# Attention and an MLP mixer on one core: batch 0 loaded by ranges of tokens, its down projection by seven block products, in a new order

## The chip, the core and the metric

The kernel runs on one core of a Trainium2 chip. The core's engines work side by side: PE (TensorE) multiplies matrices into PSUM, DVE (VectorE) and ACT (ScalarE) copy, add and exponentiate, POOL (GpSimd) and SP (SyncE) mainly issue DMA transfers. The metric is the device time of one execution in microseconds (us); smaller is better. The profile is of one execution, whose own time is given beside the times of the other runs.

## What is computed

Eight batches, eight heads, 576 tokens of 64 channels. Attention is causal in blocks of 64 tokens; its output x (576 x 512 a batch) goes through a token mixer and a channel mixer:

```python
scores = scale * q @ k^T                  # block_i >= block_j, else -1e9
x = softmax(scores) @ v                   # per head; heads side by side: [8, 576, 512]
h = relu(x^T @ w_tok1) @ w_tok2           # 576 -> 256 -> 576, over tokens
u = x + h^T
out = u + relu(u @ w_ch1) @ w_ch2         # 512 -> 1536 -> 512, over channels
```

Inputs and output are float32 in HBM.

## The kernel before

Every piece of work is registered by `P.add(engines, cost, emit, deps, ...)` and gets the next number. The string `ORDER` then says in what order the pieces are issued and on which engine: `173Tsbc` is piece 173 on PE (T), with the PSUM places s, b and c; A is ACT, D is DVE, P is POOL, S is SP. Each engine runs its own pieces in this order and waits only where a tile is not ready or not free, so a load that stands early in POOL's order delays all that POOL issues behind it. The costs in `P.add` and the fields `prio`, `xfer` and `at` served the planner that wrote the string; at run time the string alone counts.

**Loads.** `load_qk(b, hg)` brings k and q of four heads (group hg). For batches 1 to 7 POOL issues one DMA each (L413) that casts float32 to bf16. The partition is (head, 32 groups of 18 tokens), so a run in HBM is 18 tokens. DVE then transposes 32 x 32 blocks (L436) into kT and qT, where 32 partitions hold one head. The raw buffer of a group is free for the next batch only when these transposes are done. For batch 0, group 0, SP loads k in float32 in two halves (L420) into the idle tile gT[0] (`k_stage`), ACT casts them (L395 by the helper `cast`), and POOL loads q in three pieces (L431); group 1 comes by POOL in halves. `load_v` (L462) has ten loads for batch 0 (five blocks of 128 tokens for each group) and five for the others. The weights follow on POOL: w_tok1 and w_tok2 (L473), w_ch1 in eight pieces f, m (L496), w_ch2 in three (L505).

**Batch 0's attention** (`first_attention`) runs before anything else can. Group and pair j (0 to 3) have three score sets n each: set 0 holds the blocks of tokens 256 to 575 against each other, sets 1 and 2 the others. `score_set` emits matmuls of 32 rows (L560). The first set covers all four heads of group 0. ACT takes exp of 1024 columns at a time (L578). The product with v (L608, and L661 for the last 64 tokens) is divided by its sum on DVE (L628, L634). Until there is work, PE multiplies zeros (`raise_clock`: WARM = 11 matmuls, L366, and single fillers, L373).

**Token mixer of batch 0**: `token_up` (L802, L806) and `first_uT` (L835, L850), which makes u transposed, uT, directly, so that u itself is not stored for this batch.

**Channel mixer.** `channel_up` (L1021), for batch 0 alone, has 12 products of four matmuls, each followed by relu. `channel_down_fast` (L1348) makes the down projection of the batches from 1 on by seven block products on half-size blocks (84 matmuls of 256 columns, four sums of blocks on DVE at L1330, six folds with the residual u at L1372). Batch 0 has `first_down` instead: for each of four row blocks four matmuls with the identity bring the residual from uT (L1439), and twelve of 512 columns the product (L1443); a cast and a store follow. `weight_sums` (L1300) makes the sums of w_ch2 that the block products need.

**Opening.** `init_tiles` fills constants on DVE (the ones and zeros of v1, the zeros for the warm-up, the bars of the mask) and the identity on POOL, which stands late in the order (12P, behind the v loads).

Of the kernel before, what the change touches and what calls it, by code (L numbers as in the profile page):

```python
# [9 lines left out]
FP32 = mybir.dt.float32  # L10
# [17 lines left out]
class Plan:  # L28


    TURN = {
# [22 lines left out]
    def add(  # L54
        self, engines, cost, emit, deps=(), prio=0.0, take=(), give=(), xfer=None, mode=0, at=0.0,
        urgent=0, until=1e9, quick=False, stick=False,
    ):

        o = Op()
        o.engines = (engines,) if isinstance(engines, str) else tuple(engines)  # L60
        o.cost = cost if isinstance(cost, dict) else {e: cost for e in o.engines}
        o.emit, o.prio, o.take, o.give, o.xfer = emit, prio, take, give, xfer
        o.mode, o.at, o.urgent, o.until, o.quick, o.stick = mode, at, urgent, until, quick, stick
        o.deps = list({id(d): d for d in deps if d is not None}.values())
        o.n = len(self.ops)
        self.ops.append(o)
        return o
# [30 lines left out]
    13S 9D 5D 16S 1D 43Ta 21P 2D 7D 11D 19P 10D 4D 3D 23P 31P 29P 14A 25P 15D 17A 33P 22D 18D 27P 20D 44Tb 249P 45Tb  # L98
    46Tb 47Td 24D 48Ta 49Ta 37P 50Ta 173Tsbc 36P 179Tt 174A 51Ta 52Ta 35P 53Ta 54Ta 55Ta 56Ta 57Ta 180A 34P 175D
    177Ts 26D 58Ta 59Ta 30D 176P 60Ta 178A 198Tt 252P 32D 61Ta 62Ta 40P 63Ta 199A 64Ta 28D 196Ts 42P 65Ta 66Ta 67Ta  # L100
    197A 230Tt 251D 258P 68Ta 69Ta 250D 70Ta 192A 39P 71Ta 211Ts 231A 189Td 38P 185Ta 186T 190D 181Tb 191D 182T 193A
    41P 232D 215Tt 212A 194D 154P 195D 72Tc 183D 73Tc 184D 200Td 74Tc 216A 75Tc 157P 213D 217Ts 8D 233D 254D 155P
    201T 218A 234Tt 187D 188D 12P 204Tb 214D 253D 205T 235A 255P 236Ts 206D 207D 156P 202D 227Ta 237A 203D 208Tb
    160P 223Tc 228D 224T 229D 219Td 159P 220T 225D 278Taefg 226D 161P 209D 210D 246Tc 221D 158P 222D 238Tb 281A 239T
    247D 162P 248D 242Td 279A 243T 240D 336Tc 163P 241D 282A 244D 334Ta 245D 280A 165P 260D 338Tb 335D 273Tdhfg 256D
    339A 342Ta 276A 340Tb 164P 277A 348Te 343T 341D 275A 337D 349T 399P 257D 351Tb 352T 350A 259D 263P 345Tc 344A
    346T 353D 274A 266Tfghe 262P 347D 267A 298Tabdc 261P 268A 356Tf 302A 265P 301A 360Tc 300A 357D 269A 358Td 361A
    354Tb 299A 270A 310Tcagf 355D 362Th 313A 271D 303D 272P 304D 312A 330D 264P 364Tb 363A 314A 396P 376Ta 311A 166P
    331D 370Te 359A 402P 365A 167P 305Tcdgh 371A 377D 366Tb 405P 309A 6D 168P 400D 308A 368Ta 401D 307A 306A 292Tf
    321Td 369A 293D 289Te 294D 286Tc 367A 322D 324Th 323D 374Tf 290D 291D 287D 288D 315Td 375A 325D 372Te 326D 398D  # L110
    283Tc 397D 373A 327Th 295Ta 316D 317D 570P 425Tbgfe 296D 328D 409P 329D 318Td 284D 427A 285D 387Th 319D 583P
    426A 320D 297D 428A 332D 420Tcdbg 410P 429A 388T 424A 412P 423A 479Ta 333D 408P 422A 421A 411P 477Tb 404D
    413Tdcfe 585P 478D 391Tg 414A 403D 415A 407D 573P 392T 417A 406D 480A 169D 586P 393T 416A 576P 485Tb 572D
    457Tdcae 486D 378Tf 458A 170D 461A 389T 459A 171D 460A 379T 172D 390A 445Tbdca 418D 394D 487Te 446A 419D 481Th
    448A 488D 380T 449A 482D 447A 430Tb 571D 452Tcage 431D 442Td 432D 734P 456A 450D 436Th 381D 579P 455A 433Tb
    495Te 454A 483Tf 434D 435D 491Tg 453A 443D 382Ta 444D 437D 492A 451D 575D 439Tb 484D 471Td 497Tg 496D 493Tc 440D
    468Tf 498A 441D 383T 472D 574D 494D 384T 438D 469D 470D 587Tbceg 577D 385A 489Th 501D 590A 578D 474Tf 589A 465Ta
    473D 591A 740P 462Te 475D 476D 505Tcd 588A 466D 737P 463D 467D 506Tf 490A 582P 592D 520Tbg 464D 508A 502D 521Ta
    584P 507A 511T 523A 522D 499Te 509Th 512A 500D 526T 580D 510A 599Teacf 503D 527A 513T 593D 504D 603A 515T 581D
    602A 524Tb 514D 601A 651Tf 516D 600A 525A 517D 594Tcahe 652D 528T 596A 739D 530T 595A 738D 518T 598A 653Ta 529D  # L120
    904P 597A 519D 535Tcb 531D 654A 619Tdfeh 735D 538A 533T 623A 736D 539Ta 622A 534D 536Th 901P 621A 541T 540D 743P
    620A 613Te 537D 659Tg 542A 624P 545T 614D 532A 615D 750P 626Tdcfh 660D 604Te 749P 546D 629A 661Tg 605D 628A 543T
    606D 630A 548T 662D 655Te 627A 544D 664S 631Tcfhg 549A 625D 547D 657Td 656D 632A 607Ta 633A 610Tb 658D 554Tce
    635A 608D 611D 663S 634A 612D 609D 616Tb 550D 555A 648Ta 763Tdfgh 551D 386S 556T 766A 395S 552D 765A 764A 560T
    553D 767A 557D 758Tdgfh 649D 650D 642Tc 759A 558Ta 643D 760A 741D 761A 644D 617D 645Td 762A 618D 669Tgc 665D
    646D 639Tb 647D 672A 684Tfh 640D 670Td 641D 559D 675T 671A 636Tb 745D 562T 676A 917P 744D 687A 666D 916P 561D
    690T 673Td 563D 747P 691A 564T 637D 674A 638D 568S 913P 667D 742D 751Tbagf 746P 565D 677T 914P 752A 679T 753A
    678D 566T 915P 754A 680D 755A 748P 795Tbadg 567D 756P 815Tf 907P 799A 668D 905D 798A 910P 688Te 902D 797A 685Td
    903D 796A 817Ta 689A 816D 686D 692T 818A 694T 693D 681A 783Tbdgf 695D 821Ta 785A 757D 819Te 822D 786A 682T 787A
    825Td 820D 699Tag 683A 826D 829S 823Tf 784A 777Tc 702A 824D 774Td 788P 697T 789P 778D 705T 779D 698A 775D 771Tb  # L130
    830S 776D 703Te 706A 906D 790Tcdfh 772D 704A 773D 780Ta 911D 794A 700Tb 569S 791A 781D 709T 782D 701D 793A 707T
    792A 768Ta 710D 918Tcbhf 708D 827Td 920A 769D 770D 800Te 921A 828D 806Tb 919A 712T 807D 922A 831S 801D 925Tadhc
    802D 713A 909D 923P 803Tf 926A 996P 808D 851Tge 832D 928A 999P 804D 836Tab 805D 927A 852Th 854D 837Tf 833D 853A
    857T 838D 839A 809Td 855Th 929A 912D 840Tf 696D 856A 812Tc 834D 841A 842T 810D 811D 1009P 858A 861T 835D 924D
    844T 1005P 813D 814D 866Tgd 862D 859T 845D 869A 864T 843A 860D 846T 865A 872T 908D 870Ta 847D 873A 1002P
    962Tcfhe 871A 848D 867Tg 711D 965A 876T 714D 963A 849T 868A 874T 850D 966A 718Tch 964A 875D 877D 930Tbage 878D
    982Tf 719D 934A 997D 931A 879T 932A 998D 720T 983A 1000D 1094P 933A 1001D 880A 715D 950Tbaef 1097P 938Td 1011P
    952A 716D 941Tg 724T 953A 721D 951A 954A 942D 943D 957Tabce 939D 955P 940D 947Tg 717D 958A 956P 944Tf 1008P 959A
    935Td 984Ta 948D 949D 961A 1010P 945D 946D 960A 936D 1006D 1025Tgfbe 1012P 985A 937D 979Tc 1007D 1028A 967Ta
    1027A 722Td 980D 981D 1103P 968D 1026A 969D 1004D 1029A 1013Tcabf 723D 973Tg 1017A 1003D 976Te 726T 1015A 974D  # L140
    1100P 975D 1016A 977D 978D 1014A 725D 970Tg 1057Teabf 727D 1108P 728T 971D 1061A 972D 1106P 863D 1058A 881D
    1060A 1109P 1052Tgcdf 1059A 990Tb 729D 1018P 1054A 1077Ta 1019P 1056A 991D 1110P 1055A 1020Tcbef 1053A 1078D
    730T 1024A 1099D 1023A 1095D 1022A 1098D 1045Tdagf 1021A 731D 1036Tb 1049A 992Te 1102D 1046A 1030Tc 1037D 1033Th
    1096D 1048A 1079Tf 1047A 1038D 1031D 993D 1039Tb 1080A 986Td 1034D 995S 1035D 1042Ta 1032D 1089Th 1050D 1043D
    1051P 1044D 987D 1111Tcgef 1090A 1040D 1071Ta 1041D 1113A 1093S 1081Td 1072D 1115A 1062Tb 1073D 1065Th 1082D
    1112A 732S 1083Ta 1114A 1063D 1068Tg 733S 1064D 1074Tc 1066D 1069D 1116P 1118Tbdfe 1070D 1107P 1075D 1076D
    1085Tg 1067D 1121A 1084D 988Tc 1122A 1311Th 1104D 1120A 1105D 1119A 1309Ta 1101D 1312A 1086D 1150Tdbfe 989D
    1310A 885Thg 882D 1153A 994S 1154A 1152A 1143Tacfe 886D 1151A 1087Tb 1146A 1091S 887T 1144A 1088D 1147A 883D
    1145A 1123Tdabf 888D 1092S 891T 1124A 1148D 884D 1127A 1149P 1126A 1155Tcdeh 1117D 892D 1125A 1137Tf 1156A
    1134Tb 1138D 1131Ta 1157A 1139D 889Tc 1135D 1158A 1132D 1136D 1159A 1133D 1160Tb 1163Ta 1161D 1140Tf 1162D  # L150
# [28 lines left out]
def kernel(  # L179
# [11 lines left out]
    nc = tc.nc  # L191
# [73 lines left out]
    P = Plan()  # L265
# [1300 lines left out]
```

## Time and profile before

| what | value |
|---|---|
| runs | median 284.94 us of 3 (284.32 to 285.04) |
| the profiled execution | 285.06 us |
| its span, first to last instruction | 283.0 us, granted clock 0.999 |
| SP's two k loads, from issue to landing | 2.9 and 4.5 us |
| POOL's batch-0 v loads, from issue to landing | 4.4 to 5.5 us, ten of them |
| ACT's 1024-column exponentials | 11, 1031 ns each |
| fillers on PE (L366, L373) | 11 and 32 matmuls, 9.6 us |
| the last matmul starts | 279.6 us |

The span has no repeated loop that one could read once for all: the opening (0 to 20 us) is loads and batch 0's attention, then PE is full to the end while the stages of neighbouring batches overlap. "Idle before" a row is time that the engine stood still just ahead of it, with the work that ended the wait.

### The profile page before, as it was taken

The page shows a single profiled execution, that of the slowest core. Times are in us where ns is not written, and L with a number is a line of the kernel's source. Part 1 is how long each engine was busy: PE and PEld are TensorE (multiplying, and loading weights), DVE is VectorE, ACT ScalarE, POOL GpSimd, SP SyncE. Part 2 cuts the span into 40 slices and gives each one's busy share as a digit, 9 for nine tenths or more (in the row PEclk, how much of TensorE's full clock was granted, in tenths as well). Part 3 has the DMA queues.
Part 4 walks back from the last instruction along what each step waited for, and adds up shares of the span by engine and source line. Part 5 has one row for each costly group of instructions (what it writes and reads, how often), then busy time and mean ns, then how long its engine had stood idle before and what let it go on. Part 6 is the DMA issues. An engine that isn't in the chain of part 4 may idle for free.

```text
span 283.0 us, 9371 instructions
## 1 busy us (share of the span) xinstructions
PE 275.3 (97%) x4004; PEld 196.2 (69%) x4027; DVE 245.1 (87%) x533; ACT 172.3 (61%) x312; POOL 69.3 (24%) x115
## 2 busy tenths in 40 slices
PE   7899999999999999999999999999999999999995
PEld 3567565567776877887877767744488985468884
DVE  4678479799999988999999988899699898899975
ACT  3786887575998659787879687164514245734000
POOL 6895555511241090040535110000000000000000
PEclk9999999999999999999999999999999999999999
DMA  7999999994959599668599494030115603000436
GB/s 160 155 157 195 192 164 209 170 126 77 122 80 157 155 137 155 152 104 105 81 121 102 60 193 92 2 148 0 21 37 142 120 2 121 29 2 0 151 76 220
DMA packets 64776, 31.79 MB, mean 112 GB/s; under 512 B 53088, under 2 KB 55904, under 8 KB 64736
## 3 DMA queue, kind: packets, MB, share of 16 engines
q0 software_dynamic: 45040, 17.64, 54.0%
q1 hardware_dynamic: 19120, 12.78, 18.1%
q10 hardware_dynamic: 576, 0.79, 0.8%
q8 instruction: 31, 0.51, 0.7%
q14 instruction: 9, 0.07, 0.1%
HBM read 35.85 MB, written 9.44 MB: 160 GB/s over the span
## 4 chain that ended last, share of the span: by engine, by line
PE 85%; DMA 7%; POOL 3%; DVE 2%; issue 1%; ACT 0%; SPq 0%; DVEq 0%; POOLq 0%
PE late L1348 16%; PE mm L1348 10%; PE mm L1090 7%; PE late L1214 7%; PE late L1090 7%; PE mm L1214 6%; PE mm L560 6%; PE mm L608 4%; DMA wc_sb<-in_moe_w_ch_dram 4%; PE mm L802 3%; PE late L1443 2%; POOL vals L462 2%; PE mm L897 2%; PE late L608 2%; DMA vals<-in_v_dram 2%; PE mm L661 2%
## 5 line engine op out<-in xcount | busy, mean ns | idle before, releaser
L767 ACT ACTIVATE e_sb<-late 128x512 bf16<-128x512 f32 x85 | 48.4, 605 | 10.7 <-PE late L560 9.4
L767 ACT ACTIVATE e_sb<-mm 128x512 bf16<-128x512 f32 x83 | 47.1, 606 | 9.5 <-PE late L560 8.3
L436 DVE STREAM_TRANSPOSE qk_sb<-qk_sb 128x288 int32<-128x288 int32 (+1 forms) x65 | 41.3, 692 | 3.6 <-ACT qk_sb L395 1.9
L462 POOL DMA_DIRECT2D vals<-in_v_dram x45 | 36.8, 831 | 21.0 <-PE mm L661 8.8
L1348 PEld LDWEIGHTS <-gT 128*128 128x128 bf16 x288 | 27.7, 98 | 5.3 <-issue 0.9
L1348 PEld LDWEIGHTS <-sums 128*128 128x128 bf16 x288 | 27.7, 98 | 3.9 <-issue 0.7
L560 PEld LDWEIGHTS <-qk_sb 32*64 32x64 bf16 x1280 | 19.5, 104 | 13.7 <-issue 9.9
L560 PE MATMUL mm<-qk_sb 32*64 32x64 bf16 (+7 forms) x584 | 27.8, 287 | 0.3
L608 PEld LDWEIGHTS <-e_sb 128*128 128x128 bf16 x640 | 23.7, 97 | 5.1 <-issue 1.1
L560 PE MATMUL late<-qk_sb 32*64 32x512 bf16 (+7 forms) x556 | 26.4, 295 | 0.0
L1090 PEld LDWEIGHTS <-ws_sb 128*128 128x128 bf16 x192 | 18.2, 98 | 3.6 <-issue 0.9
L608 PE MATMUL mm<-vals,e_sb 128*128 128x65 bf16 x450 | 20.1, 193 | 0.1
L634 DVE TENSOR_TENSOR x_sb<-mm,rinv 128x256 bf16<-128x256 f32 x45 | 18.8, 422 | 1.3
L395 ACT COPY mm<-late 128x512 f32<-128x512 f32 (+1 forms) x15 | 8.7, 577 | 16.4 <-PE late L1348 8.0
L1348 PE MATMUL late<-wd_sb,gT 128*128 128x256 bf16 x144 | 17.7, 273 | 0.0
L1214 PEld LDWEIGHTS <-ws_sb 128*128 128x128 bf16 x96 | 9.3, 98 | 10.1 <-issue 0.2
L1090 PEld LDWEIGHTS <-wc_sb 128*128 128x128 bf16 x144 | 15.3, 114 | 1.2
L413 POOL DMA_DIRECT2D qk_sb<-in_k_dram x14 | 7.6, 543 | 33.3 <-DVE rinv L628 12.9
L788 ACT ACTIVATE gT<-mm 128x512 bf16<-128x512 f32 x19 | 11.3, 619 | 4.1 <-PE mm L1214 2.4
L788 ACT ACTIVATE gT<-late 128x512 bf16<-128x512 f32 x18 | 10.6, 601 | 4.4 <-PE late L1090 1.8
L1348 PE MATMUL late<-wd_sb,sums 128*128 128x256 bf16 x108 | 13.3, 273 | 0.0
L1214 PEld LDWEIGHTS <-wc_sb 128*128 128x128 bf16 x72 | 8.0, 113 | 7.0
(207 smaller groups left out, 644.0 us busy)
## 6 DMA issues: line engine op xcount, KB each, us to landing
out_dram<-o_sb SPq DMA_DIRECT2D x14, 512.0 KB, 3.6
qk_sb<-in_k_dram POOLq DMA_DIRECT2D x14, 288.0 KB, 4.4
qk_sb<-in_q_dram POOLq DMA_DIRECT2D x14, 288.0 KB, 5.3
vals<-in_v_dram POOLq DMA_DIRECT2D x28, 128.0 KB, 6.5
wc_sb<-in_moe_w_ch_dram POOLq DMA_DIRECT2D x8, 192.0 KB, 7.8
wc_sb<-in_moe_w_ch_dram POOLq DMA_DIRECT2D x3, 512.0 KB, 10.0
out_dram<-o_sb SPq DMA_DIRECT2D x5, 256.0 KB, 3.2
vals<-in_v_dram POOLq DMA_DIRECT2D x15, 64.0 KB, 5.0
```

What stands on the lines that cost most here:

```text
L395: nc.scalar.copy(dst, src)
L436: nc.vector.transpose(dst[:, 0:S, :] .rearrange("p s e -> p (s e)") .bitcast(I32) .rearrange("p (a k) -> p k a", k=NB)[:, k0:k1], raw2.bit ...
L462: nc.gpsimd.dma_start(out=t[128 - p : 128, J, hs, 0:64], in_=src)
L560: nc.tensor.matmul(out=home(n)[64 * half : 64 * half + 64, c : c + w], lhsT=bar[r, 0] if j is None else kT[i][r, 64 * j : 64 * j + 64, par ...
L608: nc.tensor.matmul(out=u[:, I, 0:65], lhsT=e[:, h, c : c + 128], rhs=vt[:, J, head, 0:65], start=(J == 0), stop=(J == I),)
L634: nc.vector.tensor_tensor(out=xt[:, 0:4, 64 * head : 64 * head + 64], in0=u[:, :, 0:64], in1=ri[:, 0:4].to_broadcast([128, 4, 64]), op=MULT,)
L767: nc.scalar.activation(dst, bank_of(x), EXP, scale=scale)
L788: nc.scalar.activation(dst, src, RELU)
L802: nc.tensor.matmul(out=ps, lhsT=w1_sb[:, c, tt : tt + 255 : 2], rhs=xt[:, c, cols], start=(c == 0), stop=False)
L1090: nc.tensor.matmul(out=bank_of(bank)[:, 256 * o_ : 256 * o_ + 256], lhsT=x(o_, m), rhs=y[:, :, m, :], start=opens, stop=m == 1, skip_group ...
L1214: nc.tensor.matmul(out=bank_of(bank), lhsT=x(m), rhs=y[:, :, m, :], start=first and m == 0, stop=m == 1, skip_group_check=not first,)
L1348: nc.tensor.matmul(out=bank_of(bank)[:, 256 * i : 256 * i + 256], lhsT=x[:, kk, 128 * i : 128 * i + 128], rhs=y[:, kk], start=first and i ...
```

## The change

Three edits and a new `ORDER`.

1. *Loads of batch 0, group 0.* k and q are both cut by tokens. SP loads tokens 256 to 575 in two pieces each of k and q (5 of 10 tokens of each run, 1280 bytes), all four staged in float32 and cast by ACT. POOL loads tokens 0 to 255 (`k` and `q`, one DMA each, 8 tokens a run). The source is now heads by 32 runs, because the runs of one head's range and the next head's are not evenly spaced. The first score set waits for the four near pieces alone.
2. *Opening.* The v1[0] constants move from DVE to POOL, and with the identity they stand ahead of POOL's first DMA: every POOL load has them in its `deps` (`opening`). In the new order POOL starts 12P 5P 4P 3P (identity, constants), then 29P 27P 19P 35P 33P 40P 31P 167P and so on. WARM falls from 11 to 9, and the order has 42 single fillers where 32 stood.
3. *Channel mixer of batch 0.* `first_down` goes; `channel_down_fast(0, ...)` takes its place, with `turn`, which brings the residual back from uT by the same 16 matmuls with the identity and a cast per quarter. `channel_up` is cut into halves of two matmuls that wait for two pieces of wc1 each.

```diff
+        if o.engines == ("POOL",) and xfer is not None:
+            deps = [*deps, *self.opening]
...
-    k_stage = gT[0].rearrange("p c s -> p (c s)").bitcast(FP32)
+    stage = [gT[0].rearrange("p c s -> p (c s)").bitcast(FP32)[:, 1152 * n : 1152 * (n + 1)] for n in range(2)]
...
-    WARM, KEEP = 11, 110
+    WARM, KEEP = 9, 110
...
-                "DVE", ("v", i), (-1e5 + 2, -40)[i],
+                ("POOL", "DVE")[i], ("v", i), (-1e6, -40)[i],
...
-            edges = (0, 9, 18) if not (first and n) or hg else (0, 9, 14, 18)
+            ranged = first and not hg
+            edges = (0, 5, 10, 18) if ranged else (0, 9, 18)
             for f, (k0, k1) in enumerate(zip(edges, edges[1:])):
+                w = slice(D * k0, D * k1)
+                near = ranged and f < 2
+                t0, t1, nb, b0 = (256, S, 10, k0) if near else (0, 256, 8, 0) if ranged else (0, S, NB, k0)
+                b1 = b0 + k1 - k0
+                part = hbm[:, w]
+                if ranged:
+                    part = src[b, 0:4, t0:t1].rearrange("h (p k) d -> h p (k d)", p=32)[:, :, D * b0 : D * b1]
+                if near:
+                    def emit_load(o, w=w, part=part, n=n):
+                        nc.sync.dma_start(out=stage[n][:, w], in_=part)
...
+            op = None
+            for half in range(2):
+                ms = (2 * half, 2 * half + 1)
...
+                ready = [ld for n, ld in enumerate(wc1_ready[cc]) if n % NDM in ms]
+                op = P.add(
+                    "PE", mm_cost(512, 2), emit, [op] + uT_done[ms[0] : ms[1] + 1] + ready + g_war, prio + 0.1 * cc - 0.05 * (1 - half),
+                    take=() if half else [(BANK, bank)],
+                )
...
+            def turn(row, col):
+                bank = {"covers": True}
+
+                def emit(o):
+                    for i in range(4):
+                        nc.tensor.matmul(
+                            out=bank_of(bank)[:, 128 * i : 128 * i + 128],
+                            lhsT=uT[0][:, 2 * row + i // 2, 2 * col + i % 2, :], rhs=ident,
+                            start=i == 0, stop=True, skip_group_check=i > 0,
+                        )
...
+                return P.add(EVAC, evac_cost(512), emit, [op], prio - 0.5, give=[bank])
...
+                rows_done = u_done if b else [turn(row, col)] if residual else []
...
-    qk[0, 0] = load_qk(0, 0, pads["v", 0] + pads["w1"])
+    P.opening = pads["ident"] + pads["v", 0]
+    qk[0, 0] = load_qk(0, 0)
...
-                first_down(g_done, wc2_ready, uT_done)
+                channel_down_fast(0, g_done, wc2_ready, uT_done, 4.0)
```

In the new order the down projection's products of batch 0 stand behind the score sets of batch 2 and the token mixer of batch 1, where before its parts were spread among them. The numbers of all later pieces differ, and the order of the remaining batches is new as well.

More of the change, by code (lines that the diff above doesn't have):

```diff
@@ L28 @@
 class Plan:
+    opening = ()
     TURN = {
@@ L103 @@
[L103 to L127, printed above, removed]
@@ L356, in emit @@
             make_identity(nc, ident)
-        pads["ident"] = [P.add("POOL", 0.6, emit, (), -90)]
+        pads["ident"] = [P.add("POOL", 0.5, emit, (), -2e6)]
     def raise_clock():
@@ L702, in first_attention @@
     def first_attention(ready, v_ready):
+        near = [op for i, op in enumerate(ready[0]) if i % 3 < 2]
         pad = pads["v", 0]
@@ L721, in first_attention @@
                     op = score_set(
-                        0, hg, n, range(4), ready[hg], prio - 0.05, [(SC, note)] + [(BANK, x) for x in early]
+                        0, hg, n, range(4), near, prio - 0.05, [(SC, note)] + [(BANK, x) for x in early]
                     )
```

216 lines of the change are left out of this document (104 added, 112 removed).

## The prediction

> **What bounds the kernel now.** The page's first lines and the table of engine time by stretches come first:
>
> ```profile
> span 283.0 us, 9371 instructions
> PE 275.3 (97%) x4004; PEld 196.2 (69%) x4027; DVE 245.1 (87%) x533; ACT 172.3 (61%) x312; POOL 69.3 (24%) x115
> ...
> 8.00:20.00 12.00, 11.55 (x263) 7.26 (x264) 8.08 (x25) 11.01 (x13) 11.13 (x20) 1.00 1.49 153
> 20.00:30.00 10.00, 9.77 (x277) 7.56 (x278) 8.17 (x26) 6.75 (x14) 6.51 (x11) 1.00 1.13 192
> 60.00:80.00 20.00, 19.79 (x357) 14.81 (x360) 18.90 (x52) 15.22 (x31) 4.46 (x7) 1.00 0.63 83
> ```
>
> The columns are the stretch and its length, then busy time of PE, PEld, DVE, ACT, POOL, the granted clock, DMA share and GB/s. From 20 us on PE is full, so time is won only by less PE work or by PE filling earlier. Before 20 us "busy" misleads: 11 matmuls of L366 and 32 of L373 multiply zeros to hold the clock. So the opening is read from the chain of waits and from the timeline:
>
> ```profile
> 1.22 4.51 DMA gT<-in_k_dram
> 5.74 0.68 ACT qk_sb L395
> 6.45 0.73 DVE qk_sb L436
> 7.46 0.53 POOL qk_sb L413
> ...
> 14.03 0.72 POOL vals L462
> 14.75 5.14 DMA vals<-in_v_dram
> ...
> 19.93 0.65 PE mm L661 x20
> ```
>
> ```profile
> 8.00 0.33 PE L560 MATMUL sc<-qk_sb 32*64 32x320 bf16 x2 [1.18 <-DVE qk_sb L436]
> 8.76 1.02 ACT L578 ACTIVATE e_sb<-sc 128x1024 bf16<-128x1024 f32 x1 [2.35 <-PE sc L560]
> 19.93 0.46 PE L661 MATMUL mm<-vals,e_sb 128*64 128x65 bf16 x8 [0.45 <-DMA vals<-in_v_dram]
> 26.33 0.38 PE L850 MATMUL mm<-w_sb,aT 128*128 128x512 bf16 x1
> ```
>
> The first scores start at 8.00 because the second k piece lands late. ACT's exponentials start at 8.76 and fill ACT to 20.55. Then PE waits for a load of v at 19.93. The first use of w2 (26.33) comes just after w2 lands: issued 19.41, 6.6 us to landing, 26.0. The trace's records of single DMA packets say why the loads are late: POOL's queue is one line that is never empty from 3.59 us to past 30. Times between the first packets of successive loads (us):
>
> ```
> first packet of POOL's first load 3.59, of the last v of batch 0 18.64
> q of heads 0 to 3 (3 loads) 1.89; q, k of heads 4 to 7 0.71 each
> v of four heads, 128 rows 0.65; q or k of batch 1 1.75; a piece of wc1 0.98
> ```
>
> By these prices the line up to the last v is 1.89 + 4 x 0.71 + 8 x 0.65 + 3 x 1.75 = 15.2, against 18.64 - 3.59 = 15.05 measured. So after SyncE's loads this line sets the opening, not the moment of the first scores.
>
> **The parts of the change.** *Down projection.* 48 matmuls of 512 columns go; 0.86 us for four in the chain (L1443), 0.215 each, 10.3 us. In come 7 x 2 x 6 = 84 of 256 columns; 1.31 for 12 (L1348), 0.109 each, 9.2. The 16 products with ident stay 16, now in turn. The seed's bank was last given back as "full", so no cover matmul is added. **-1.15 us on PE**, which is the bound. DVE and ACT gain work: four sums (0.95 each, L1330), a seed (0.6), four casts in turn (0.6 to 0.69), six folds (0.68, L1372) against four casts before. On DVE that is 3.8 + 4.1 + 0.7 less 1.4; but the new list gives ACT and POOL other copies and memsets (three seeds of the down projection, six tail operations and the like), and counted at its rows DVE nets +3.4 us, ACT some +5. I cost these at nothing: ACT has 110 us free, DVE 38. Without that cover it is rival D.
>
> *Halves of the up projection.* 12 products of four matmuls become 24 of two: the same 48, no cost; a half can start on two pieces of wc1.
>
> *SyncE's four pieces.* Four issues at 0.41 us (L420) end at 0.75 + 1.64 = 2.4. In the packet records 2304 bytes take 93 ns and 4 bytes 9, so a run of 1280 is estimated at 56 ns; 512 of them on 16 engines are 1.8 us. After the slow first half microsecond (1.79 to 2.3) they end at 4.1; landing was seen 0.65 after the last packet (3.06 to 3.71), cast 0.46 (0.67 for 576, less 256 columns at ACT's rate), transpose 0.48 (the row of 128x160), 5.7. On PE, zeros is now the fourth memset of DVE, so the warm-up starts at 1.6, runs 9 x 0.43 to 5.4, then six fillers at 0.11: **first scores at 6.1 instead of 8.0**. ACT needs the far tokens for its fourth exponential, and they are second and third in POOL's line.
>
> *POOL's opening.* ident (0.57 us from 18.11 to 18.68) and three memsets (about 0.7, from POOL's own memset rows of 0.1 to 0.3) now stand ahead of its first DMA, which moves from 1.25 to some 2.3. All its other loads queue behind, and ACT, DVE and PE wait for those. But before, that DMA's first packet came at 3.59, in the nanoseconds in which the first engine ended SyncE's second piece; a single issue at 61.79 has its first packet 1.25 later. So packets could flow from 3.55, and what holds them is SyncE's own end on the engines, later by 1.8 - 1.5 (32 runs of 56 ns against 16 of 93): **the line starts 0.3 us later, at 3.9.**
>
> *POOL's line.* Counting the calls of P.add tells which load each number is. New line up to the last v (43P): two far loads (2048 bytes read, 0.65 each between the rows), four of heads 4 to 7, wc1 piece 167 moved ahead of nine v loads, three loads of batch 1, the same v: 1.3 + 2.84 + 0.98 + 5.25 + 5.2 = 15.6 against 15.2. The last v is **0.3 + 0.4 = 0.7 us later**, 20.6. Before, POOL also stood still for 1.57 us ahead of the load at 7.46, for the transposes of k; the line had work meanwhile, so losing that wait wins nothing. Ahead of its v wait PE now has one score set of batch 1 and the end rows of j=1 more behind it, some 0.6 us: the shift there is 0.1. Behind the v the line is as before (w1, one load of batch 1, w2), so w2 lands at 26.7. There PE has 0.3 us less done than before at 26.33 (a token product and a transpose less, a score set more): 0.4 + 0.3 = **+0.7 us**. Bounds: if the lead of 1.9 us of the first scores carries through, -1.9; if the far loads go at the price of 144 KB loads, and POOL's memsets hold the line until 4.3, +1.4. I take +0.7, since w2 is the row that ended last; at the pieces of wc1 the total of the line is as before and nothing more is lost.
>
> *The new list for the rest* (another order from 30 us on): the gaps between matmul starts beyond their columns' time sum to 5.8 us from 30 us on; an order may win or lose about an eighth of them, so -0.7 to +0.7; I take 0.
>
> Sum: -1.15 + 0.7 = -0.45. The profiled execution took 285.06 us, a span of 283.0 and 2.1 around it; it is 0.12 above the median of 284.94. 284.94 - 0.45 = **284.5 us**.
>
> **A rule against the change.** In the trace 14 to 16 packets of SyncE's k loads are under way at once between 2.4 and 3.6 us. The Trainium skill, DMA: Bandwidth & Descriptors, section "Why a DMA increments its semaphore by 16 and not by 1", says that a DMA is spread over the largest number of engines, up to 16, that divides the slowest dimension of both sides. By that rule, the new pieces, whose source is 4 heads by 32 runs, would go over 4 engines; the whole k loads, whose 128 runs are evenly spaced, over 16, with which the trace agrees. No row here has a source with so short an outer dimension; rival C is what it would do.
>
> **The rivals.** *B, the lead carries* (chance 0.19): v and w2 do not end last, and PE fills 1.9 us earlier. For it: PE waited only 0.45 us for v at 19.93, and ACT is the fuller engine until 20.55. Against: the line's sum. 284.94 - 1.15 - 1.9 = 281.9.
>
> *C, few engines* (0.14): the four pieces run on four engines, 128 runs of 56 ns each, 7.2 us, to 9.5; with landing, cast and transpose the first scores are at 11.3, 3.3 late, and ACT's 11.8 us of exponentials end 3.3 after 20.55, less 0.6 of work done ahead: 284.94 - 1.15 + 2.7 = 286.5. If POOL's packets interleave, the last k packets of before stood 152 ns apart, and it is 4 or more: 288 and over. It decides from any count under about 10 engines. For it: the 128 runs no longer lie at one distance. Against, weakly: the v loads, 4 heads by 128 rows, do spread, but their outer side is the rows.
>
> *D, the other side: DVE at the batch-0 folds* (0.14). Between 60 and 80 us DVE has 20 - 18.9 = 1.1 us free, and the new sums and folds fall at some 55 to 65. If the net 3.4 us land there, 2.3 do not fit, the folds give their banks back late, and PE waits: 284.5 + 2.3 = 286.8. It decides once that stretch holds over 20 us of DVE work. Against: 40 to 60 has 3.2 free.
>
> *E, no effect* (0.05): the opening takes back the 1.15, 284.9.
>
> **How the numbers follow.** Forecast 0.48, B 0.19, C 0.14, D 0.14, E 0.05. A measurement of this kernel tells about 0.3%, 0.85 us, from no change: under 284.1 is faster, over 285.8 slower. The forecast's own range is 283.0 to 286.2, 0.21 faster, 0.16 same, 0.11 slower. B adds 0.19 faster, E 0.05 same, C 0.14 slower, D 0.12 slower and 0.02 same: 0.40, 0.23, 0.37. The range from 282.2 to 287.2 leaves out about half of B, half of C and a little of D.
>
> **What would show it.** First scores near 6.1 and ACT's first exponential near 6.9; POOL's first DMA near 2.3; PE waiting for vals to about 20.6; the first L850-type product near 26.7; 84 matmuls more in the 256-column groups of the down projection and none of first_down; DVE near 248 us. The forecast is wrong if the first scores are later than 8 (C), if no wait for vals or w_sb stands before 27 us (B), or if PE shows waits for folds after 50 us (D).

## The result and the profile after

The changed kernel took a median of 299.26 us (four runs, 297.93 to 300.35), the kernel before 284.99 beside it: a ratio of 1.0503, interval 1.0449 to 1.0557. The forecast was 284.5, with a range to 287.2. The profiled execution took 298.47 us, 13.6 us of span more than before. A few executions run at a lower granted clock and some per cent longer; the times below leave them out, and of the profiled executions of e1, e2 and e5 (0.95 over the whole span; e5 has no other) only the first 16 us are read. The page and the table by stretches of the changed kernel (columns as before: busy PE, PEld, DVE, ACT, POOL, granted clock, DMA share, GB/s):

```profile
span 296.6 us, 9524 instructions
...
PE 278.4 (94%) x4071; PEld 202.1 (68%) x4071; DVE 246.3 (83%) x530; ACT 175.4 (59%) x320; POOL 72.8 (25%) x123
```

```profile
8.00:20.00 12.00, 4.73 (x82) 3.27 (x83) 4.94 (x13) 3.38 (x6) 4.32 (x7) 0.57 0.84 125
20.00:30.00 10.00, 9.86 (x200) 6.26 (x199) 3.77 (x15) 9.25 (x10) 6.59 (x12) 1.00 1.29 134
60.00:80.00 20.00, 20.00 (x378) 15.38 (x377) 19.39 (x38) 12.53 (x25) 10.71 (x15) 1.00 1.56 178
```

The loss is in the row from 8 to 20: ACT has 3.4 us of work where it had 11.0, PE 4.7, and at a clock of 0.57. From 60 to 80 us PE is full. The timeline of the changed kernel shows why (start, length, engine, line, operation; in brackets the idle time before and what ended it):

```profile
0.75 0.75 SPq L432 DMA_DIRECT2D gT<-in_q_dram  x1
...
2.17 0.69 POOL L443 DMA_DIRECT2D qk_sb<-in_k_dram  x1
...
2.74 0.74 SPq L432 DMA_DIRECT2D gT<-in_k_dram  x1
...
5.56 0.46 ACT L399 CAST qk_sb<-gT 128x320 bf16<-128x320 f32 x1 [3.53 <-DMA gT<-in_q_dram]
...
7.28 0.46 ACT L399 CAST qk_sb<-gT 128x320 bf16<-128x320 f32 x1 [1.26 <-DMA gT<-in_k_dram]
...
11.61 0.46 ACT L399 CAST qk_sb<-gT 128x320 bf16<-128x320 f32 x1 [3.87 <-DMA gT<-in_q_dram]
...
14.27 0.46 ACT L399 CAST qk_sb<-gT 128x320 bf16<-128x320 f32 x1 [2.20 <-DMA gT<-in_k_dram]
...
15.27 0.47 PE L572 MATMUL sc<-qk_sb 32*64 32x320 bf16 x2 [9.16 <-DVE bar L344]
...
16.31 0.55 POOL L417 DMA_DIRECT2D qk_sb<-in_q_dram  x1 [6.31 <-DVE qk_sb L448]
...
16.44 1.02 ACT L590 ACTIVATE e_sb<-sc 128x1024 bf16<-128x1024 f32 x1 [1.72 <-PE mm L572]
```

SP's four pieces are issued by 3.5 us and arrive one after the other: each bracket of a cast is a wait for one more piece, 1.7 us apart at first and then 4.3 and 2.7. The first scores start at 15.27 in place of 8.00, after PE has idled for 9.16 us. (The row names `bar`, a memset that stands behind the last transpose in DVE's order; what is late is the piece.) POOL, in order too, stands for 6.31 us before its first load of batch 1, whose buffer these transposes have to free; the last v of batch 0 lands at 28.0 us (20.1 before) and w2 at 35.8 (26.0).

The table follows the difference through the kernel. The third column is experiment e4, which has the old loads in the new kernel. Starts in the profiled executions, us:

| | before | after | e4 |
|---|---|---|---|
| first scores | 8.00 | 15.27 | 7.04 |
| last score matmul of batch 0 | 19.10 | 28.77 | 19.00 |
| last score matmul of batch 7 | 172.90 | 183.49 | 174.09 |
| last matmul | 279.59 | 291.08 | 281.68 |
| end of the span | 283.0 | 296.6 | 287.0 |

After minus e4 is 8.2, 9.8, 9.4, 9.4, 9.6: what the loads cost is complete at 29 us, and nothing comes to it later. e4 minus before is -1.0, -0.1, 1.2, 2.1, 4.0: the new order loses slowly, and 1.9 us at the very end. The -1.0 is no gain of the new order: 8.00 is high for these loads. In the profiled execution before, the last five k packets ran one by one, 152 ns apart, until 5.34 us; in seven other profiles with the same two k loads (e4, e7, e8, e9, e14, e15, e16; e9 and e14 are built from the kernel before) the last one ends at 3.9 to 4.0, and the first scores start at 6.8 to 7.3.

### The profile page after: what moved, and what is told of

The parts are those of the page before. It is cut to its first block, busy times and chain, and to the rows that moved or that the text cites. A ratio compares the mean times of both kernels' runs of the same rounds, so it can differ in the third digit from the quotient of the medians.

```text
span 296.6 us, 9524 instructions
## 1 busy us (share of the span) xinstructions
PE 278.4 (94%) x4071; PEld 202.1 (68%) x4071; DVE 246.3 (83%) x530; ACT 175.4 (59%) x320; POOL 72.8 (25%) x123
## 4 chain that ended last, share of the span: by engine, by line
PE 86%; issue 1%; ACT 1%; DVE 0%
PE mm L1369 16%; PE late L1369 12%; PE late L1111 7%; PE mm L572 7%; PE late L1235 6%; PE mm L1235 6%; PE mm L1111 5%; PE mm L620 4%; PE late L620 3%; PE late L815 3%; PE mm L910 2%; PE mm L815 2%; PE mm L1038 2%; PE late L572 2%; PE late L910 2%; PE late L1038 1%
## 5 line engine op out<-in xcount | busy, mean ns | idle before, releaser
L448 DVE STREAM_TRANSPOSE qk_sb<-qk_sb 128x288 int32<-128x288 int32 (+2 forms) x66 | 40.9, 681 | 11.5 <-ACT qk_sb L399 11.5
L572 PE MATMUL mm<-qk_sb 32*64 32x512 bf16 (+7 forms) x526 | 28.8, 295 | 0.9 <-issue 0.9
L572 PE MATMUL late<-qk_sb 32*64 32x64 bf16 (+7 forms) x614 | 29.1, 291 | 0.6 <-ACT e_sb L590 0.4
L399 ACT COPY late<-late 128x512 f32<-128x512 f32 (+1 forms) x14 | 7.9, 566 | 24.4 <-PE late L1111 9.4
L1111 PEld LDWEIGHTS <-wc_sb 128*128 128x128 bf16 x144 | 15.1, 114 | 2.1 <-issue 0.4
L1369 PE MATMUL mm<-wc_sb,gT 128*128 128x256 bf16 x132 | 16.2, 273 | 0.0
L572 PE MATMUL sc<-qk_sb 32*64 32x512 bf16 (+7 forms) x140 | 7.3, 312 | 9.2 <-DVE bar L344 9.2
L1369 PE MATMUL mm<-wd_sb,gT 128*128 128x256 bf16 x120 | 14.7, 273 | 0.0
L399 ACT COPY mm<-mm 128x512 f32<-128x512 f32 (+1 forms) x14 | 8.1, 578 | 9.5 <-PE mm L1369 6.1
L417 POOL DMA_DIRECT2D qk_sb<-in_q_dram x14 | 7.7, 553 | 23.4 <-ACT e_sb L780 13.8
```

Source lines behind the costliest of these rows:

```text
L399: nc.scalar.copy(dst, src)
L448: nc.vector.transpose(dst[:, t0:t1, :] .rearrange("p s e -> p (s e)") .bitcast(I32) .rearrange("p (a k) -> p k a", k=nb)[:, b0:b1], raw2.b ...
L572: nc.tensor.matmul(out=home(n)[64 * half : 64 * half + 64, c : c + w], lhsT=bar[r, 0] if j is None else kT[i][r, 64 * j : 64 * j + 64, par ...
L1111: nc.tensor.matmul(out=bank_of(bank)[:, 256 * o_ : 256 * o_ + 256], lhsT=x(o_, m), rhs=y[:, :, m, :], start=opens, stop=m == 1, skip_group ...
L1369: nc.tensor.matmul(out=bank_of(bank)[:, 256 * i : 256 * i + 256], lhsT=x[:, kk, 128 * i : 128 * i + 128], rhs=y[:, kk], start=first and i ...
```

## Experiments

Times are medians, each beside runs of the kernel before on the same chip (284.6 to 285.4 us).

### The old loads in the new kernel

```diff
-            edges = (0, 5, 10, 18) if ranged else (0, 9, 18)
+            edges = (0, 9, 18) if not (first and n) or hg else (0, 9, 14, 18)
...
-        near = [op for i, op in enumerate(ready[0]) if i % 3 < 2]
+        near = ready[0]
...
# e4 only: the identity and the constants of v1 stand behind POOL's eighth load
-    P.opening = pads["ident"] + pads["v", 0]
+    P.opening = []
```

> The changed kernel with the loads, casts and transposes of batch 0's first four heads as before (k by SP over two pieces of whole rows, q by POOL in three pieces, all five transposes ahead of the first scores); ident and the pads of v still come first on POOL; the new order, the halved up projection and the seven block products stay. Theory A (the loads cost it all): first scores at 8.5 to 9.5 (q waits for POOL's opening, 0.9 us), time 284 to 286. Rival C (the new order costs on its own): first scores the same, time 288 or above. The seven products by themselves are to be worth 1.15 us.

> As the run before, but POOL issues its loads first and makes ident and the pads of v after its eighth DMA. Theory A: first scores at 8.0 as in the kernel before, time 283 to 284.5, below the kernel before by the 1.15 us of the seven products. Rival C (the order costs): 286 or above. Rival D (the folds and casts of the block products hold PE up): 285 to 286 with new idle time of PE between 60 and 110 us.

e3 took 289.3 us (ratio 1.0151, 1.0110 to 1.0193), e4 288.23 (1.0105, 1.0070 to 1.0140). So 10 of the 14 us belong to the loads, and 11 to the loads and POOL's opening together. Theory A's times were too low: with first scores at 7.21 and 7.04 us, as early as in other profiles with these loads, the two are still 3 to 4 us slower than the kernel before. Theory C, that the new order costs on its own, holds beside A.

### Few engines, or POOL's queue?

e1 and e2 make every DMA of the near pieces one of 32 rows (e2 with runs twice as long, half as many), e5 leaves the four pieces and keeps POOL quiet, e6 is e2 with q's four issued by ACT:

```diff
-                        nc.sync.dma_start(out=stage[n][:, w], in_=part)
+                        for h in range(4):
+                            nc.sync.dma_start(out=stage[n][32 * h : 32 * h + 32, w], in_=part[h])
...
# e5, ahead of POOL's first load, which now stands behind the four casts in the order
+                                    nc.gpsimd.tensor_copy(gate[:, 2 * m + g : 2 * m + g + 1], near)
...
# e6
+                            (nc.scalar if n else nc.sync).dma_start(
+                                out=stage[n][32 * h : 32 * h + 32, 0 : 10 * D], in_=whole[h]
+                            )
```

> The changed kernel, but each of SP's four near pieces is issued as four DMAs, one for each head (32 rows of 1,280 B each), so 16 issues in place of 4; bytes, casts, order and everything else unchanged. Theory A (the four pieces lie on few DMA engines, and that sets the first scores): a DMA of 32 rows can use all engines, so many more than 4 packets of SP's queue are under way at once, 16 semaphore packets for each DMA; the price is 16 issues of 0.41 to 0.6 us, the last at 7 to 10 us, landed some 2 us later; first scores at 10.5 to 13 in place of 15.3, and the time falls by 3 to 6 us, to 293 to 296. Rival B (the wait is for POOL's opening or for sharing the engines with POOL's queue, and not for the number of engines): still about 4 packets or 27 packets a microsecond, first scores at 15 or later, time 299 or above.

> The changed kernel, but SP loads tokens 256 to 575 of each head and tensor as one DMA (32 rows of 2,560 B): eight issues, the two casts of a tensor both wait for its four. Theory A (few engines): last issue at 3.6 to 5, landed at 5.8 to 7.5, first scores at 7.5 to 9.5 in place of 15.3, PE keeps its full clock in 8 to 20 us, time down by 7 to 11 us, to 288 to 292; what is left over 284 is POOL's queue (its two far loads and its order). Rival B (POOL's opening and its traffic): first scores at 13 or later, time 296 or above. Rival C (the new order after the start is what costs): first scores early, but the time stays at 294 or above.

> The changed kernel with SP's four near pieces as they are, but POOL issues none of its loads before the four casts of those pieces are done (small POOL copies that read the cast columns stand ahead of its first load). Theory A (4 engines set the rate even alone): 512 packets at the 72 to 76 a microsecond that the changed kernel's trace shows before POOL's queue is busy take 7 us, last landing at 9.5 to 10, first scores at 11 to 11.5 in place of 15.3. Theory B (it is only POOL's traffic that slows SP's queue): the packets run faster than that, landed by 6, first scores at 7.5. If the wait was neither, first scores stay at 15. The time says little, since all of POOL's loads are 6 us later: 296 to 305.

> The changed kernel, but tokens 256 to 575 come as one DMA for each head and tensor (32 rows of 2,560 B), k's four issued by SP and q's four by ACT, with ACT's table load right behind them: the eight are issued by 2.7 us. Theory B (SP's queue is slow where it meets POOL's queue, so it has to be through before POOL's first packets at 3.6 to 4.0): all packets are done by 4.5, first scores at 6.5 to 8, time 286 to 290, near that of the old loads (288 to 289). Theory A' (such short runs are slow whatever the queue does): landed after 9 as with SP alone, first scores at 12 or later, time 296 or above.

| | most packets of SP's queue under way | first scores | time |
|---|---|---|---|
| changed kernel | 6 | 15.27 | 299.26 |
| e1, 16 issues | 13 | 15.52 | 298.32 |
| e2, 8 issues | 17 | 13.52 | 298.24 |
| e5, four pieces, POOL quiet | 6 | 11.74 | not read (one run, 307.31) |
| e6, two queues | 16 | 9.00 | 292.54 |

The packet records of SP's queue, counted by the microsecond in which they start (POOL's first packet comes at 3.6 to 4.2 us, in e5 at 13.0):

```
us from            1   2   3   4   5   6   7   8   9  10  11  12  13
before, 2304 B    13 118 119   4   2
changed, 1280 B    0  12  50  76  75  67  29  30  27  27  27  43  49
e1, 1280 B        24  66  38  51  31  31  23  35  36  41  47  64  25
e5, 1280 B         0  16  54  70  77  78  75  75  63   4
e6, 2560 B, both   9 116  68  59   4
```

Two things work together. In e5 four pieces alone run at 75 packets a microsecond with about 4 under way on the mean, where the loads before ran at 118 longer ones with up to 20. Its timeline has the casts evenly 1.7 us apart:

```profile
5.54 0.46 ACT L399 CAST qk_sb<-gT 128x320 bf16<-128x320 f32 x1 [3.51 <-DMA gT<-in_q_dram]
...
7.28 0.46 ACT L399 CAST qk_sb<-gT 128x320 bf16<-128x320 f32 x1 [1.28 <-DMA gT<-in_k_dram]
...
9.01 0.46 ACT L399 CAST qk_sb<-gT 128x320 bf16<-128x320 f32 x1 [1.27 <-DMA gT<-in_q_dram]
...
10.73 0.46 ACT L399 CAST qk_sb<-gT 128x320 bf16<-128x320 f32 x1 [1.27 <-DMA gT<-in_k_dram]
...
11.74 0.47 PE L577 MATMUL sc<-qk_sb 32*64 32x320 bf16 x2 [5.02 <-DVE bar L344]
```

That is 3.7 of the 7.3 us (4.7 of 8.2 against e4's first scores). The other 3.5 are POOL's: its queue moves 27 to 59 KB a microsecond from 4 to 7 us and 125 to 182 from 7 to 11, and there SP's rate falls from 75 packets a microsecond to between 27 and 30. The four engines also show in the completions. By the view of the DMA queues from 0 to 16 us, first before, then after (packets, MB, share of the engines' time):

```profile
q1 hardware_dynamic: 288, 0.59, 11.6%
```

```profile
q1 hardware_dynamic: 528, 0.66, 12.8%
```

Before, 256 packets of data and 32 of completion for two DMAs, 16 each; after, 512 and 16 for four DMAs, four each. The rule of the Trainium skill that the prediction weighed (DMA: Bandwidth & Descriptors, "Why a DMA increments its semaphore by 16 and not by 1") says just that, and the trace agrees.

But e1 undoes the four engines, with 16 completions for each DMA, and wins little (1.0462, 1.0415 to 1.0508; e2 1.0443, 1.0394 to 1.0493), so theory A's numbers missed in both, and first scores came as late as rival B had them (15 and 13 us or later). The 16 issues of e1 reach to 9.3 us, and from 5 to 11 us POOL's queue leaves it 23 to 41 packets. In e2 the last packet ends at 9.4, 4.5 us before that of the changed kernel, but its first cast then waits 1.28 us for a table load on ACT besides. Only e6, where all eight DMAs are issued by 2.6 us, is done by 5.4, before POOL's bulk, and that wins 6.7 us of the time (1.0254, 1.0219 to 1.0288), though 292.54 is above the 286 to 290 that theory B had. Its casts still start only at 6.71, and all four stand in a row ahead of the first scores:

```profile
6.71 1.54 ACT L398 CAST qk_sb<-gT 128x320 bf16<-128x320 f32 x4 [2.58 <-DMA gT<-in_q_dram]
...
9.00 0.47 PE L575 MATMUL sc<-qk_sb 32*64 32x320 bf16 x2 [2.59 <-DVE bar L343]
```

No run has spread pieces of 1280 bytes with POOL quiet, so the two causes are not measured apart in every combination. The same page of the Trainium skill has, in "Queues, rings and completion order", that each engine goes round robin between the queues it has packets for; the fall from 75 to 27 agrees in kind, and no run here shows the order on one engine.

### The half clock after the wait

```diff
# e11: 68 more filler matmuls of 256 columns ahead of the first scores (177Tsbc)
# e12: all 42 fillers with 512 columns, and all ahead of the first scores
-                    out=bank_of(bank)[:, 0:256], lhsT=zeros[:, 0:128], rhs=zeros[:, 0:256],
+                    out=bank_of(bank), lhsT=zeros[:, 0:128], rhs=zeros,
```

> The changed kernel with 68 more filler matmuls (256 columns, 0.107 us each at full clock) on TensorE ahead of the first scores, so that it works through 7 of the 9 us in which it waits; loads and everything else unchanged. Theory K (part of the loss is the granted clock, 0.50 to 0.67 from 8 to 20 us after 9 us of idling): the clock stays at 0.9 or above from 8 to 20 us, first scores as before at 15.3, first attention done 1.5 to 2.5 us earlier, time 296.5 to 298 in place of 299.3. Rival (scores and exps there wait for the loads, so that the clock costs nothing): 299 or above.

> The changed kernel; its 42 filler matmuls have 512 columns in place of 256 and all stand ahead of the first scores, none between the first attention's sets; the number of TensorE's instructions is the same. 42 x 0.213 = 8.9 us of work fills the wait from 5.8 to 15.3 us. Theory K (the half clock after the wait costs the 1.7 us by which the run with 68 more fillers ended its first attention earlier, and that run was slower only because its 136 more instructions moved the fetches of TensorE's instructions to places where TensorE ran dry: 1.5, 2.0 and 2.75 us at 37.8, 53.7 and 105.9 us): clock 1.0 from 8 to 20 us, no gaps beyond those of the changed kernel, time 1.3 to 2 us less, 297.3 to 298. Rival W (working through the wait costs in itself, as the later loads then collide with an earlier attention): 299 or above with gaps that name a wait.

Both missed: e11 took 301.17 us (1.0528, 1.0482 to 1.0574), e12 299.62 (1.0528, 1.0492 to 1.0563). By stretches, e11 and then e12:

```profile
8.00:20.00 12.00, 10.31 (x148) 7.81 (x146) 4.80 (x13) 5.04 (x8) 4.48 (x7) 1.00 0.89 131
20.00:32.00 12.00, 11.45 (x272) 7.33 (x270) 7.31 (x27) 9.96 (x13) 10.16 (x19) 1.00 1.34 152
```

```profile
8.00:20.00 12.00, 9.99 (x112) 4.83 (x111) 5.14 (x13) 4.43 (x7) 4.49 (x7) 1.00 0.90 133
20.00:32.00 12.00, 11.26 (x229) 7.68 (x224) 5.34 (x18) 8.26 (x10) 9.63 (x19) 0.57 1.25 144
```

In e11 the clock holds in this stretch, and batch 0's last product with v comes at 33.04 us, 1.7 earlier than in the changed kernel: the size of the clock's cost there. It fits the clock records of the changed kernel, which have 0.50 from 8.4 to 18.7 us, 3.4 us of it behind the first scores: at half the clock that is 1.7 us of work lost. In e11 it is lost again in gaps at 38, 54 and 106 us, which the last part takes up, and in a stretch of half clock from 56.0 to 59.4 us behind the second of them. In e12 the fillers missing between the score sets leave gaps of 1.16 and 0.80 us, to 17.57 and 19.46, and the half clock only comes later, from 21.2 to 31.5. So neither way of filling the wait won the 1.7 us.

### The seven products by themselves

e9 puts them by hand into the old order, e10 also makes the identity ahead of POOL's loads; e15 instead takes them out of the new order, with e16 (the same as e7, below) as its partner in one call:

```diff
# e9, e10 (from the kernel before); e15 is the reverse in e7
-                first_down(g_done, wc2_ready, uT_done)
+                channel_down_fast(0, g_done, wc2_ready, uT_done, 4.0)
```

> The kernel before, with its loads and its order, and of the change only the down projection of batch 0: seven block products, four sums, four turned blocks and seven folds stand in the places of the order where the 48 wide matmuls and their four casts stood; the up projection stays whole. Prediction (the products save 1.15 us of TensorE and hide their DVE work): 283.5 to 284 where the kernel before has 284.6 to 285, ratio 0.995 to 0.997. Rival D (3.4 us more of DVE at its busiest place holds TensorE up): 285 to 287. Theory O (it is the rest of the new order that cost 3 us in e4): as the prediction says, so that 4 us lie between this kernel and e4.

> As e9, with ident made first on POOL, so that POOL's loads start 0.6 us later. In the kernel before the last 5 packets of SP's k load ran between POOL's packets until 5.4 us, and the second k cast waited for them until 5.74. Theory B (SP's queue is slowed where it meets POOL's): k has landed by 4.5, first scores at 7.2 to 7.5 in place of 8.0, time 0.3 to 0.7 us below e9. Rival (q, the first of POOL's queue, is what the first scores wait for): first scores at 8.2 or later, time 0.2 to 0.6 us above e9.

> As e7 (old loads, old opening, new order, 21 wide fillers), but batch 0's down projection is the old one: 48 matmuls of 512 columns and four casts stand in the places of the new order where the 84 of 256 columns, the sums, the turns and the folds stood; the halved up projection stays. Prediction's first term (the seven products save 1.15 us of TensorE; by the starts of the matmuls in the traces 1.0 to 1.4): 0.9 to 1.5 us slower than e7 in the same call. Rival D (their DVE work costs as much): the same as e7 within 0.4 us, or faster.

> e7 again, on the same chip as the run before it, to compare the two: 287.2 to 288.2 us.

e9 took 294.56 us (1.0316), e10 292.16 (1.0239). PE's waits in e10 from 44 to 80 us (line, what for, us in all, times, longest):

```profile
PE late L1369 <- ACT u_sb L394: 1.4, 1, 1.4
...
PE late L1347 <- ACT late L394: 0.7, 1, 0.7
PE mm L983 <- DVE u_sb L911: 0.7, 1, 0.7
PE mm L559 <- DVE x_sb L633: 0.6, 1, 0.6
```

The turns share one bank and wait for ACT's casts, and the products for the seed: these runs measure the places chosen by hand, not the products. e9 also had the half clock (0.72 from 20 to 32 us, 0.58 from 57 to 61, 0.57 from 78 to 82), where e10 holds 1.00 from 19 to 82. They do show that the DVE and ACT work is not hidden in any place: the new order, in e4, has no such wait from 30 to 280 us. What e10 was to show of k missed too: k's last packet ends at 4.0 us already in e9, and the first scores came at 7.28 there and at 7.75 in e10; e10 is still 2.4 us faster, which goes with its clock and was not traced further. e15 took 290.75 us against 287.86 for e16: without the products 2.9 us more. In both profiles PE has one long gap near 100 us, e15 first:

```profile
PE mm L561 <- issue: 2.0, 1, 2.0
```

```profile
PE late L1101 <- DMA uT<-u_sb: 1.9, 1, 1.9
```

They cancel, and the last matmul comes 2.2 us later in e15. Its instructions on PE are fewer, so that their transfers (next section) fall elsewhere too. The terms can be read in the traces without a run. Adding for each line the time from each matmul's start to the next one's start, all down projections take 74.59 + 1.13 + 10.20 = 85.9 us before and 83.61 + 0.90 = 84.5 after.

### The late end and gaps without a wait

```diff
# e7 (from e4) and e13 (from the changed kernel): every second filler left out, the others with 512 columns
# e8 (from e4): the stores of tokens 512 to 575 of batches 4 to 7 left out
-                    op = P.add(("SP", "ACT"), 0.5, emit, [folded[row, h] for h in range(2)], prio, xfer=8 * 0.086)
+                    op = P.add(("SP", "ACT"), 0.5, emit if row == 0 else lambda o: None, [folded[row, h] for h in range(2)], prio, xfer=8 * 0.086)
# e14 (from the kernel before): 4 in place of 11 wide matmuls, 70 more fillers of 32 columns
-    WARM, KEEP = 11, 110
+    WARM, KEEP = 4, 110
```

> The changed kernel with the old loads and the old opening of POOL (e4), and 21 of the 42 filler matmuls of the start left out while the other 21 have 512 columns in place of 256: 42 fewer instructions on TensorE, the same work. Theory F (the last stores are late because a 16 KB transfer of the queue of kind instruction, which came at 281.6 us in that run and not at all at the end of the kernel before, holds one of the 16 engines): no such transfer in the last 10 us, last store landed 1.75 us after its issue and not 3.6, time 1.7 to 1.9 us less, 286.3 to 286.5. Theory S (too many bytes of stores at the end): time as before this edit, 288.2.

> As e4, without the two stores of the last rows of batches 4 to 7 (tokens 512 to 575), 256 KB each, that come at 277.8 us on SP and ACT at once: that part of the output is left out. Theory S (the end is late because 1.5 MB of stores are issued in its last 10 us, where the kernel before has 1.0 MB in that time): the last store lands 1.75 to 2.2 us after its issue in place of 3.6, time 1.4 to 1.9 us less. Theory F (the instruction transfer): still 3 us or more to landing, time 288.

> The changed kernel with every second one of its 42 filler matmuls left out and the other 21 with 512 columns: the same TensorE work in 42 instructions less. Theory G (TensorE runs dry for 1.2 us at 106.8 us because a 16 KB transfer of the queue of kind instruction, issued at 105.5, comes late for a stretch of short instructions; another such transfer falls among the last stores): the transfers come at other places, no gap over 0.9 us after 20 us, no transfer among the stores, time 1.5 to 2.5 us less, 296.8 to 297.8. Rival (gaps are waits for data, and the end is set by the bytes of the stores): 299 or above.

> The kernel before with 4 in place of 11 wide matmuls at its start and 70 more narrow ones (32 columns) before its first scores: about the same work there, but all that follows stands 126 instructions of TensorE later, half of the 256 between two of its instruction transfers. Theory G (the gaps come from where these transfers fall, whatever the kernel): its transfers fall half a step elsewhere, one or more gaps of 0.9 us or more appear where short instructions follow a transfer, and the last transfer may fall among the last stores; time 286 to 288.5. Rival (the kernel before is not sensitive to that): within 0.5 us of the kernel before.

| | before | after | e4 | e7 | e8 | e13 | e14 |
|---|---|---|---|---|---|---|---|
| time | 284.99 | 299.26 | 288.23 | 287.72 | 287.62 | 297.82 | 286.53 |
| from DVE's last fold to the end of the span | 2.7 | 4.8 | 4.6 | 3.8 | 3.3 | 4.0 | 2.7 |
| last store, issue to landing | 1.75 | 3.45 | 3.63 | 2.82 | 2.16 | 2.66 | 1.75 |

From the view of DMAs of the changed kernel, 288 to 297 us, and of the kernel before, 275 to 283:

```profile
q8 instruction: 1, 0.02, 0.7%
q14 instruction: 1, 0.01, 0.2%
...
out_dram<-o_sb ACTq DMA_DIRECT2D x2, 256.0 KB, 4.2
```

```profile
out_dram<-o_sb ACTq DMA_DIRECT2D x2, 256.0 KB, 2.0
```

Without the 16 KB transfer (e7) the end is 0.8 us shorter than in e4, without the two stores (e8) 1.3: both theories hold in part, and together they cover the 1.9. The expectation of e8 counted wrongly: both kernels issue 1.5 MB of stores in their last 10 us; what the new order changed is that the two are issued at once on both queues, 3.9 us ahead of the last matmul, and not in turn by SP 4.9 and 4.3 ahead. These are ends of single profiled executions. In the times they can't be told from the spread: e4's ratio is 1.0105, that of e7 1.0122 and, run again as e16, 1.0074 (1.0043 to 1.0105), that of e8 1.0107 (1.0085 to 1.0129).

The other part are gaps of PE that name no wait ("issue"). From the timeline of the changed kernel, then of e11:

```profile
107.98 0.22 PE L572 MATMUL mm<-qk_sb 32*64 32x64 bf16 x2 [0.95 <-issue]
```

```profile
55.78 0.22 PE L623 MATMUL mm<-vals,e_sb 128*128 128x65 bf16 x2 [1.84 <-issue]
...
108.70 0.42 PE L623 MATMUL late<-vals,e_sb 128*128 128x65 bf16 x8 [2.56 <-issue]
```

Each ends 1.25 to 1.6 us after the end of a 16 KB transfer of the queue of kind instruction (106.7, 54.3 and 107.1 us). In e13, 42 instructions shorter, the gap without a name is gone, but in its place stands a wait for data:

```profile
109.04 0.66 PE L1109 MATMUL late<-uT,wc_sb 128*128 128x256 bf16 x4 [0.87 <-DMA uT<-u_sb]
```

e13's end is 0.8 us shorter; its ratio of 1.0477 (1.0439 to 1.0515) is not clear of the changed kernel's 1.0503. e14 does not decide: it is slower (1.0056, 1.0024 to 1.0089), but its one gap over 0.9 us, from 29.85, waits for a piece of wc1, and no transfer fell in its last 7 us.

No version here beats the kernel before; the nearest with any of the change is e7, with 287.72 and 287.86 us in its two calls.

## Why the prediction was wrong

- **SP's four pieces** is the step that failed: "512 of them on 16 engines are 1.8 us", first scores at 6.1. They came at 15.27. The pieces ran on four engines (3.7 us by e5, 4.7 against e4's first scores), and SP's queue had to share them with POOL's (3.5 more). The step had also taken it that the pieces were through before POOL's line began; its own numbers, an end at 4.1 and a line from 3.9, left no room for a slower end. The lead of 1.9 us itself was counted from the 8.00 of one execution; against the 6.8 to 7.3 of other profiles with these loads it was 0.7 to 1.2.
- **Rival C** named the mechanism, and its 11.3 for four engines alone (its terms add up to 11.1) stands against 11.74 in e5. Its price was too small and its chance too low. It called the interleaving "4 or more: 288 and over"; it was 7.3 late. The weak argument against it, that v loads of 4 heads by 128 rows do spread, came from POOL's queue and another shape.
- **What a long wait costs besides** was not priced: half clock after it (1.7 us by e11), and POOL's line standing for 6.31 us.
- **POOL's opening** held: its first load at 2.17 (2.3 forecast), first packets at 4.0 (3.9). **POOL's line** failed with the first step: last v at 28.0, not 20.6, since its load of batch 1 waits for transposes that come 8 us later.
- **Down projection**: -1.15 forecast, 85.9 - 84.5 = 1.4 us in the traces, 2.9 in e15 against e16; where the further 1.5 comes from was not traced. DVE grew by 1.2 us (245.1 to 246.3) and not 3.4, and rival D did not come: no wait for folds after 50 us. **Halves**: 10.64 to 10.77 us on PE, nothing.
- **The new list for the rest**, "-0.7 to +0.7; I take 0", failed too: e4 is 3.2 us slower than the kernel before by the medians and 4.0 by the spans, although its first scores are 1.0 earlier and its products shorter by 1.0 (84.9 us in its trace). So 6.0 us are to be found in the spans. Of them 1.9 are the end, 1.3 the gap at 97 us, and 1.3 fillers behind the first scores (4.7 us in e4, 3.4 before), by which the lead is gone before 19 us. The score sets' 34.3 us of PE in e4 against 32.6 before hold the gap at 97 us, and are 0.4 apart without it. The rest is spread over several lines and was not traced to one cause. The estimate looked at gaps that an order can close, and not at the stores and the instruction transfers that it can move.

## What to carry to other kernels

A load that the first work waits for needs more than an early issue: count the engines that its shape lets it use, and let all its packets be through before a second queue starts. If it cannot be spread in few issues, split the issues over two queues, as e6 did, rather than issue more of them on one; here the old loads of whole rows, with first scores at 6.8 to 7.3, stayed ahead of e6's 9.00. A new order should be read at its two ends and at its transfers of instructions as well as in its middle.

## What the hardware showed unexpectedly

- Spreading in 16 issues did not help by itself: e1's pieces had 16 completions each and up to 13 packets under way, and still only 23 to 41 packets a microsecond beside POOL's queue, where the four-engine pieces alone had 75.
- TensorE's instructions come in 16 KB transfers of 0.9 to 2.2 us, 31 or 32 of them in an execution of some 8,100 recorded instructions of PE. In the fifteen profiles that are read beyond 16 us, PE has eight gaps over 0.85 us after 20 us that name no wait: one each in the changed kernel, e4, e6, e8 and e15, and three in e11. All eight end 1.25 to 1.65 us after the end of such a transfer: at 107.98 in the changed kernel (transfer's end 106.73), 98.60 in e4 (96.95), and 39.24, 55.78 and 108.70 in e11 (37.86, 54.32, 107.11). The Trainium skill, Runtime: NRT & Kernel Launch, section "Instruction fetch mechanics", has these blocks of 256 instructions and calls the cost of a boundary mostly hidden; the size agrees, and here it was hidden at most boundaries, and cost 0.89 to 2.56 us at these eight. That the transfer is the cause is inferred from the times and from e13; it was not tried by itself.
- The length of a gap alone did not decide the clock. In e12, gaps of 1.16 and 0.80 us within 3 us were followed by a clock of 0.50 from 21.2 to 31.5 us, with PE busy from 24 us on; in e11 one of 1.84 us, to 55.78, by 0.50 from 56.0 to 59.4. Gaps of 1.34 us in e4, 2.03 in e15 and 2.56 in e11 (to 108.70) were followed by the full clock. In e9 gaps of 1.42 and 0.87 us came shortly ahead of the half clock at 57 and 78 us; e10 has the same gaps at the same lines, 1.42 and 0.86, and kept its full clock.
